# The last matrix product by seven products of halves, and input products in pairs of units

## The chip, the cores and the metric

One core of a Trainium2 chip runs the whole program. The metric is the time of one execution in microseconds (us) of device time. The engines are TensorE (PE, with its weight loads shown as PEld), VectorE (DVE), ScalarE (ACT), GpSimd (POOL) and SyncE (SP), which issues the transfers.

## The reference

Attention over 2 batches, 12 heads, 448 positions and head size 64 gives a matrix x of 896 tokens by 768. Two experts follow:

```python
scores = np.where(mask, -1e9, scale * q @ k.T);  x = softmax(scores) @ v
h = x @ w_in;  x = (h - np.tanh(h)) @ w_out              # first expert, d_ff 2048
a = x @ w_a;   b = x @ w_b;   out = (a * b) @ w_out2     # second expert, d_ff 1536
```

Everything is float32. The weights arrive as 8-byte words, whose bits the kernel unpacks on the chip.

## The kernel before

**Precision.** Each float32 operand is split into a high and a low half in the fp32r type: ACT casts the high half (`wh<-t`, line 244, for weights; line 601 for activations), DVE subtracts to get the low half (line 253; line 602). A product of two such operands takes three matmuls (high by high, high by low, low by high), all issued in line 280. A matmul covers 128 rows of depth, 128 output rows and 448 token columns, which are one batch.

**Weights.** SP loads a tile of 768x128 weights in two transfers (line 170). ACT casts its upper bits (`top<-raw`, line 179), DVE puts the bits together (`t<-raw,top`, line 193), and then the tile is split as above. The weight buffers hold five pairs of split tiles ahead of PE.

**Seven products.** Where a product is done on a 2x2 grid of blocks (two output blocks by two depth halves of the weights, two depth halves by two batches of the tokens), it takes seven block products instead of eight. They carry the numbers 1, 2, 5, 3, 6, 7, 4. The sums of blocks that they need are DVE work: `combine` for weights (lines 213 to 219), `minus` for tokens (line 605). A *unit* is one such 2x2 grid of weights. Each of the seven products of a unit of the second expert's input is 9 matmuls. The results stay in PSUM banks (tags s, o, t, h), into which later products of the unit go on adding. Before that, ACT copies some of them out (line 733), and DVE adds (line 697).

**Second expert, input.** Twelve units (six of w_a, six of w_b, in turn). `in_turn` sets the order of their products: unit after unit, 2, 6, 5, 7, 3, 4, with product 1 of the next unit ahead of 4. `times` (line 722) multiplies a by b into twelve g tiles.

**Second expert, output.** 768 output columns are six blocks, taken two at a time. Of the depth of 1536, the first 768 go by the seven products (`seven`), the second 768 by ordinary products (`rest`): for each two blocks 7x9 + 4x18 = 135 matmuls. The tokens' terms for it come from `early_terms`, `late_terms` and `split_wide`; `kept` (line 858) copies a result out of PSUM, and `put` stores it.

The order of the instructions from the first expert on is set by the framework's scheduler, which moves instructions that are ready ahead of others on each engine. On the chip every engine works through its own list in order.

Of the kernel before, what the change touches and what calls it, by code (L numbers as in the profile page):

```python
# [9 lines left out]
F32 = mybir.dt.float32  # L10
F32R = mybir.dt.float32r
# [40 lines left out]
def attention_moe_moe2(ctx, tc, q, k, v, w_in, w_out, w_a, w_b, w_o, out):  # L52
# [20 lines left out]
    PARTS = KD  # L73
    NK = KD // 2
    WB = 5
    scale = 1.0 / float(D) ** 0.5

    const = ctx.enter_context(tc.tile_pool(name="const", bufs=1))
# [30 lines left out]
        units.append(len(tiles))  # L109
        tiles.extend([block(w, slice(0, DM), f), block(w, slice(0, DM), f + 1)])  # L110

    def in_turn(u0, early):

        n = len(units) - u0
        out = [(0, 1), (0, 5), (1, 1), (1, 5)] if early else [(0, 1)]
        for u in range(n):
            ms = [2, 5, 6, 3, 7, 4] if early and u == n - 1 else [2, 6, 5, 7, 3, 4]
            for m in ms:
                if m == 4 and u + 1 < n:
                    out.append((u + 1, 2 if early and u == 0 else 1))  # L120
                out.append((u, m))
        seen = set()
        stages.append([(u0 + u, m) for u, m in out if not ((u, m) in seen or seen.add((u, m)))])
        plan.extend(stages[-1])

    f0 = 0
    for g in GROUPS1:
# [9 lines left out]
        for dm in range(KD) if f0 < DFF1 // 128 else DM_ORDER:  # L137
            whole(block(w_out, slice((f0 - g) * 128, f0 * 128), dm))
    u0 = len(units)
    for f in range(0, NF2, 2):  # L140
        for w in (w_a, w_b):
            pair(w, f)
    in_turn(u0, True)
    for dm in range(0, KD, 2):
        pair(w_o, dm)
        u = len(units) - 1
        plan.extend((u, m) for m in (1, 5, 2, 3))
        whole(block(w_o, slice(DM, 2 * DM), dm))
        plan.extend((u, m) for m in (6, 7))
        whole(block(w_o, slice(DM, 2 * DM), dm + 1))  # L150
        plan.append((u, 4))
    last_use = {}
    for j, (i, m) in enumerate(plan):
        for x in (i,) if m is None else (units[i], units[i] + 1):
# [3 lines left out]
    thirds, summed = {}, set()  # L158

    def load_part():  # L160

# [20 lines left out]
    def bits():  # L182

        i = at["bits"]
        while at["t"] in last_use and last_use[at["t"]] < at["halve"]:
            at["t"] += 1
        if i >= at["abs"] or i >= at["t"] + TP:
# [4 lines left out]
        ts[i] = tp.tile([128, KD, 128], I32, tag="t", name="t")[:, 0:nk]  # L192
# [3 lines left out]
        at["bits"] += 1  # L196

    def source(j):

        i, m = plan[j]  # L200
        if m is None:
            return ts[i].bitcast(F32)
        if m == 7:
            return thirds[i]
        t = ts[units[i] + int(m in (4, 5))].bitcast(F32)
        return t[:, 3:6] if m in (2, 3, 4) else t[:, 0:3]

    def combine(u, m):
# [5 lines left out]
        elif u not in summed:  # L214
# [3 lines left out]
            nc.vector.tensor_tensor(out=a21, in0=a21, in1=a22, op=ALU.add)  # L218
            nc.vector.tensor_tensor(out=a11, in0=a21, in1=a11, op=ALU.subtract)

    def split_high():
        j = at["high"]
        if j >= len(plan):
            return
        i, m = plan[j]
        full = m is None
        if not full and j > at["halve"]:
            return
        if (i if full else units[i] + int(m not in (1, 2))) >= at["bits"]:
# [7 lines left out]
        if m in (3, 5, 6, 7):  # L237
# [472 lines left out]
    def times(u, q, x, on_chip):  # L710

        f, b = u // 2 * 2 + q // 2, q % 2
        if u % 2 == 0:
# [3 lines left out]
                x = e  # L717
            left[q] = x
            return
        if f not in g32:  # L720
            g32[f] = g_full[0].tile([128, NT], F32, tag=("gwh", "gwl")[f // NK if f < KD else f % 2], name="g32")
        nc.vector.tensor_tensor(out=g32[f][:, BATCHES[b]], in0=x, in1=left.pop(q), op=ALU.mult)

    def turn(u, m, outcome):

# [5 lines left out]
        if m in (1, 6, 5):  # L731
            c = {1: c1, 6: c2, 5: z}[m][u] = etile()
            nc.scalar.copy(out=c, in_=o)  # L733
        elif m == 4:
            outcome(u, 2, o, False)
        else:
# [55 lines left out]
            for _ in terms:  # L792
                pass

    last, wide = [{} for _ in range(NK)], {}

    def early_terms(kk):

        g1, g2 = g32[kk], g32[kk + NK]
        t = [partp.tile([128, NT], F32R, tag="part", name="gpart") for _ in range(2)]  # L800
        last[kk][1], last[kk][5] = [[x[:, cs] for x in t] for cs in BATCHES]
        halve(*last[kk][1], g1[:, B0])
        minus(g1[:, B0], g1[:, B1], g1[:, B0])
        halve(*last[kk][5], g1[:, B0])
        minus(g1[:, B1], g2[:, B1], g1[:, B1])

    def roomy(f):

        if f == NF2 - 1:
            return small(2)  # L810
        pool, tags = (xp, ("xh", "xl")) if f < KD + NK else (xtra, ("th", "tl"))
        t = [pool.tile([128, NT], F32R, tag=x, name=x) for x in tags]
        return [[x[:, cs] for x in t] for cs in BATCHES]

    def split_wide(cs):

        for f in range(KD, NF2):
            if f not in wide:
                wide[f] = roomy(f)
            halve(*wide[f][cs.start // S], g32[f][:, cs])  # L820

    def late_terms():

        for kk in range(NK):
            t = [xp.tile([128, NT], F32R, tag=x, name=x) for x in ("xh", "xl")]
            last[kk][2], last[kk][3] = [[x[:, cs] for x in t] for cs in BATCHES]
        for m, cs in ((2, B0), (3, B1)):
            for kk in range(NK):
                halve(*last[kk][m], g32[kk + NK][:, cs])
        for kk in range(NK):  # L830
            g2 = g32[kk + NK]
            minus(g2[:, B1], g2[:, B1], g32[kk][:, B0])
            minus(g2[:, B0], g2[:, B0], g2[:, B1])
        split_wide(B0)
        for kk in range(NK):
            last[kk][7], = small()
            halve(*last[kk][7], g32[kk][:, B1])
        for m, cs in ((6, B1), (4, B0)):
            for kk in range(NK):
                t = g_full[0].tile([128, NT], F32R, tag="gwh", name="gwh")  # L840
                last[kk][m] = [t[:, x] for x in BATCHES]
                halve(*last[kk][m], g32[kk + NK][:, cs])
            if m == 6:
                split_wide(B1)

    def seven(o, m, go_on=False, done=1):

        wh, wl = next_weights()
        product(o, [((wh[:, kk], wl[:, kk]), last[kk][m]) for kk in range(NK)], go_on=go_on)
        at["done"] += done  # L850
        advance()

    def rest(w, o, cs, go_on=True):
        product(o, [((w[0][:, f - KD], w[1][:, f - KD]), wide[f][cs.start // S]) for f in wide], go_on=go_on)

    def kept(o):
        r = etile()
# [12 lines left out]
    for dm in range(0, KD, 2):  # L870
        o1, o5, o2, o3 = [next_bank()[:, :S] for _ in range(4)]
        seven(o1, 1)
        r0 = kept(o1)
        seven(o5, 5)
        r3 = kept(o5)
        seven(o2, 2)
        seven(o5, 3, True)
        w = next_weights()
        rest(w, o2, B0)
        add(r0, o2)  # L880
        put(dm, B0, r0)
        seven(o1, 6, True, 0)
        r1 = kept(o1)
        rest(w, o5, B1)
        add(r1, o5)
        put(dm, B1, r1)
        at["done"] += 3
        advance()
        seven(o1, 7, True)
        add(r3, o1)  # L890
        w = next_weights()
        rest(w, o3, B1, False)
        add(r3, o3)
        put(dm + 1, B1, r3)
        seven(o1, 4, True, 0)
        rest(w, o1, B0)
        put(dm + 1, B0, kept(o1))
        at["done"] += 4
        advance()
        advance()  # L900


_INS = ["q", "k", "v"]
# [24 lines left out]
```

## Time and profile before

| | us |
|---|---|
| median of 3 runs (lowest, highest) | 558.43 (558.07, 561.26) |
| the profiled execution's own time | 559.96 |
| its span, from the first instruction to the last | 558.2 |
| PE busy | 548.0 (98%) |
| DVE busy | 425.1 (76%) |
| ACT busy | 331.0 (59%) |

PE's busy time counts overlapping matmuls once. The attention takes the first 110 to 120 us, the first expert runs until about 318 us, the second expert's input product from there to the 480s (its end and the last product's start are interleaved), the last product to 554.9 us. A last copy and a last store end the span. The granted clock of PE is 1.00 throughout, the higher of its two levels (2.4 GHz).

### The profile page before, as it was taken

To read this page: it belongs to the slowest core of one execution; us is meant where nothing else is said; L and a number is where in the kernel's file an instruction comes from. 1 tells how busy PE (TensorE), PEld (TensorE's weight loads), DVE (VectorE), ACT (ScalarE), POOL (GpSimd) and SP (SyncE) were. 2 spreads that over 40 slices of the span, in tenths; PEclk is the share of its full clock that TensorE was granted. 3 is DMA by queue.
4 is the path that set the end of the run, shared out by engine and by line. 5 is a ranking of instruction groups with operands and counts; after the bars stand their busy time and mean duration, and the time that the engine had idled before them with its cause. 6 is when DMAs were issued, how large, how long until landed. Compare 5 with 4: busy or idle time off the path is not lost.

```text
span 558.2 us, 8730 instructions
## 1 busy us (share of the span) xinstructions
PE 548.0 (98%) x3121; PEld 486.3 (87%) x3121; DVE 425.1 (76%) x876; ACT 331.0 (59%) x706; POOL 65.8 (12%) x88
## 2 busy tenths in 40 slices
PE   8999999998999999999999999999999999999997
PEld 4777788897999899899899889999999999999996
DVE  6897886479988867549879988979788699985311
ACT  6997996457677843238756464665554558754120
POOL 5688672200000000000000000000000000000000
PEclk9999999999999999999999999999999999999999
DMA  8825350067133742313741115335343533432001
GB/s 259 249 83 150 89 147 1 1 189 225 56 115 116 234 129 86 112 57 99 218 136 57 54 60 178 112 106 169 104 132 105 169 100 100 138 109 90 34 33 49
DMA packets 70827, 64.94 MB, mean 116 GB/s; under 512 B 13952, under 2 KB 70784, under 8 KB 70784
## 3 DMA queue, kind: packets, MB, share of 16 engines
q1 hardware_dynamic: 70784, 64.40, 37.0%
q8 instruction: 24, 0.39, 0.3%
q14 instruction: 19, 0.16, 0.1%
HBM read 61.63 MB, written 2.75 MB: 115 GB/s over the span
## 4 chain that ended last, share of the span: by engine, by line
PE 90%; DVE 3%; DMA 3%; ACT 2%; issue 1%; SPq 0%; DVEq 0%; ACTq 0%
PE s L280 37%; PE t L280 20%; PE h L280 13%; PE o L280 8%; PE o L432 4%; PE s L371 4%; PE t L406 3%; ACT p L392 1%; DMA raw<-in_moe_w_out 1%; PE t L451 1%; PE h L406 1%; DVE xsum L637 1%; DVE t L193 1%; DMA v<-in_v 1%; DMA raw<-in_moe_w_in 1%
## 5 line engine op out<-in xcount | busy, mean ns | idle before, releaser
L244 ACT CAST wh<-t 128x384 fp32r<-128x384 f32 (+2 forms) x154 | 81.9, 562 | 86.0 <-PE s L280 37.7
L179 ACT CAST top<-raw 128x768 f16<-128x768 bf16 (+1 forms) x70 | 73.8, 1054 | 44.7 <-DVE t L193 11.8
L253 DVE TENSOR_TENSOR wl<-t,wh 128x384 fp32r<-128x384 f32 (+2 forms) x149 | 87.0, 605 | 17.4 <-ACT wh L244 17.2
L193 DVE SCALAR_TENSOR_TENSOR t<-raw,top 128x768 int32<-128x768 int32 (+1 forms) x70 | 68.8, 985 | 4.0 <-ACT top L179 3.7
L280 PE MATMUL s<-xl,wh 128*128 128x448 f32 x150 | 55.0, 367 | 0.0
L280 PE MATMUL s<-xh,wl 128*128 128x448 f32 x150 | 54.7, 366 | 0.0
L280 PE MATMUL s<-xh,wh 128*128 128x448 f32 x150 | 54.2, 367 | 0.2 <-ACT e L733 0.2
L392 ACT ACTIVATE p<-p,m 112x448 f32<-112x448 f32 (+3 forms) x96 | 49.9, 524 | 5.6 <-DVE m L383 5.3
L697 DVE TENSOR_TENSOR e<-s,e 128x448 f32<-128x448 f32 x33 | 20.4, 620 | 31.8 <-PE s L280 31.5
L383 DVE CUSTOM_DVE_ANT_0 p<-s,mask 112x448 f32<-112x448 f32 (+3 forms) x96 | 37.9, 441 | 7.3 <-PE s L371 6.7
L280 PE MATMUL s<-gwl,wh 128*128 128x384 f32 (+2 forms) x96 | 34.9, 365 | 0.3 <-DVE gwl L558 0.3
L280 PE MATMUL s<-gwh,wl 128*128 128x384 f32 (+2 forms) x96 | 34.9, 365 | 0.0
L280 PE MATMUL s<-gwh,wh 128*128 128x512 f32 (+2 forms) x96 | 34.3, 364 | 0.0
L280 PEld LDWEIGHTS s<-xh,wh 128*128 128x128 f32 x150 | 28.2, 188 | 2.9 <-ACT e L733 0.6
L280 PEld LDWEIGHTS s<-xh,wl 128*128 128x128 f32 x150 | 28.2, 188 | 2.3
L280 PEld LDWEIGHTS s<-xl,wh 128*128 128x128 f32 x150 | 28.2, 188 | 2.3
L406 PE MATMUL t<-ident,p 112*112 112x112 f32 x195 | 27.6, 265 | 0.2 <-POOL qkh L351 0.2
L432 PE MATMUL o<-pt,v 112*64 112x224 f32 (+1 forms) x288 | 26.7, 326 | 0.9 <-DMA v<-in_v 0.9
L414 ACT COPY pt<-t 112x448 f32<-112x448 f32 (+1 forms) x39 | 18.4, 483 | 14.8 <-PE t L406 12.8
L432 PEld LDWEIGHTS o<-pt,v 112*64 112x64 f32 x288 | 19.1, 136 | 8.3 <-issue 1.1
L280 PE MATMUL h<-xh,wh 128*128 128x448 f32 x69 | 25.8, 374 | 0.0
L280 PE MATMUL h<-xh,wl 128*128 128x448 f32 x69 | 25.7, 372 | 0.0
(213 smaller groups left out, 1442.2 us busy)
## 6 DMA issues: line engine op xcount, KB each, us to landing
raw<-in_moe_w_out SPq DMA_DIRECT2D x48, 383.2 KB, 3.8
raw<-in_moe_w_in SPq DMA_DIRECT2D x32, 383.2 KB, 4.2
raw<-in_moe_w_a SPq DMA_DIRECT2D x24, 383.2 KB, 3.9
raw<-in_moe_w_b SPq DMA_DIRECT2D x24, 383.2 KB, 3.7
raw<-in_moe_w_out SPq DMA_DIRECT2D x12, 255.5 KB, 4.3
qk<-in_q SPq DMA_DIRECT2D x12, 224.0 KB, 3.3
qk<-in_k SPq DMA_DIRECT2D x12, 224.0 KB, 4.0
v<-in_v SPq DMA_DIRECT2D x24, 112.0 KB, 3.5
```

The source lines that it names most:

```text
L179: nc.scalar.copy(out=tops[i % len(tops)][:, 0:nk, :, 1], in_=top[:, :, :, 2])
L193: nc.vector.scalar_tensor_tensor(out=ts[i], in0=low[:, :, :, 0], scalar=13, in1=top, op0=ALU.logical_shift_right, op1=ALU.bitwise_or)
L244: nc.scalar.copy(out=halves[j][0], in_=x)
L253: engine.tensor_tensor(out=lo, in0=source(j), in1=hi.bitcast(F32), op=ALU.subtract)
L280: nc.tensor.matmul(o, a, b_, start=j == 0 and not go_on, stop=j == n - 1, skip_group_check=True)
L371: nc.tensor.matmul(sc[i, c][e], a[r, 0, cs], b_[r, 1, :n], start=x == 0, stop=x == len(terms) - 1)
L383: nc.vector.tensor_tensor_reduce(out=p[:, e], in0=s, in1=mask[:QC, S - n:], scale=-scale, scalar=3.0e38, op0=ALU.add, op1=ALU.min, accum_o ...
L392: nc.scalar.activation(out=p[:, e], in_=p[:, e], func=ACTF.Exp, bias=least[i][:, c, e:e + 1], scale=-1.0, accum_out=sums[i][:, c, e:e + 1],)
L406: nc.tensor.transpose(out=pst[:QC, x * QC:(x + 1) * QC], in_=blk, identity=ident[:QC, :QC])
L414: nc.scalar.copy(out=out_, in_=in_)
L432: nc.tensor.matmul(o[64 * e:64 * e + 64, cs], vt[:, k_, e, :], p.rearrange("s c q -> s (c q)"), start=k_ == 0, stop=k_ == 2 * h + 1, skip_ ...
L697: nc.vector.tensor_tensor(out=x, in0=o, in1=x, op=ALU.add)
```

## The change

The last product takes all of its depth by seven products. Its unit is now one 2x2 grid of 768x128 tiles, so each of the seven is 18 matmuls; three units cover the six output blocks. The product number is the outer loop (`for m in LAST: for n, u in enumerate(quads)`): product 1 for the three units, then product 2 for the three, and so on. The tokens' terms are made by `term()`, 21 in all, each a cast and a subtraction over 896 columns, 12 of them after a `minus` over 896 columns; three come before the last unit's product 7, one after the input products, and the others one to three at a time behind the last product's own steps. Six of the twelve weight tiles of the last product are loaded and unpacked among the last units of the input product, into the buffers called part.

The input products of the second expert run in pairs of units: each of the seven products for one unit and then for the other. In the first pair the order is 1, 5, 2, 3, 6, 7, 4, in the others 1, 2, 5, 6, 3, 7, 4.

```diff
-    def in_turn(u0, early):
+    def in_turn(u0, pairs_):
...
+        if pairs_:
+            out = [(v, m) for u in range(0, n, 2) for m in (PAIR_FIRST if u == 0 else PAIR) for v in (u, u + 1)]
...
+    LAST = (1, 2, 5, 3, 6, 7, 4)
...
     for f in range(0, NF2, 2):
         for w in (w_a, w_b):
             pair(w, f)
+            n = len(units) - 1 - u0 - FIRST_LAST
+            if 0 <= n < KD:
+                of_last(n // 2, 1, n % 2, "part")
     in_turn(u0, True)
-    for dm in range(0, KD, 2):
-        pair(w_o, dm)
...
+    plan.extend((u, m) for m in LAST for u in quads)
...
+    def combine_quad(u, m):
...
+        if m == 3:
+            less(quad(u, 1, 1), quad(u, 2, 1), quad(u, 1, 1))
+            less(quad(u, 1, 2), quad(u, 1, 2), quad(u, 1, 1))
+        elif m == 7:
+            less(quad(u, 1, 1), quad(u, 2, 2), quad(u, 1, 1))
...
+    def term():
...
+        x = {1: b11, 2: b21, 5: b11, 3: b22, 6: b11, 7: b12, 4: b21}[m]
+        if m == 5:
+            minus(b11, b12, b11)
...
+        t = [pool.tile([128, NT], F32R, tag=x, name="last") for x in tags]
+        halve(*t, x)
+        last[m, p] = t
...
+    def all_of(u, m, o, go_on=False):
...
+        parts = [((wh[:, k], wl[:, k]), [x[:, BATCHES[k % 2]] for x in last[m, k // 2]]) for k in range(KD)]
+        product(o, parts, go_on=go_on)
+        at["done"] += 2
...
     for u, m in stages[-1]:
-        if u - u0 == NF2 - 1 and m in (2, 5, 6):
-            early_terms({2: 0, 5: 1, 6: 2}[m])
         turn(u, m, lambda u, q, x, on_chip: times(u - u0, q, x, on_chip))
-    late_terms()
...
+        if u - u0 == NF2 - 1 and m == 3:
+            for _ in range(NP):
+                term()
+    last_turned.append(True)
+    term()
+    acc = {}
+    for m in LAST:
+        for n, u in enumerate(quads):
+            if m in (1, 2, 5):
+                acc[n, m] = bank({1: "sss", 2: "tto", 5: "sht"}[m][n])[:, :S]
+            o = acc[n, {6: 1, 7: 1, 4: 1, 3: 5}.get(m, m)]
+            all_of(u, m, o, m in (3, 6, 7, 4))
+            if m == 1:
+                c1[n] = kept(o)
+            elif m == 2:
+                add(c1[n], o)
+                put(2 * n, B0, c1[n])
+            elif m == 5:
+                z[n] = kept(o)
...
+            for _ in range(AHEAD[n]):
+                term()
+            advance()
```

PE's list has 2977 matmuls and transposes before and 2950 with the change; all that goes away is in the last product, 405 before and 378 now. On DVE, 878 instructions become 857.

At the start of the second expert's input product, PE's list before reads as follows. `s<-x` is at first the end of the first units' product 5, whose result ACT then copies out; the last row here is the first matmul of product 3 into the same bank, which waits for that copy.

```order
L280 MATMUL s<-xl,wh 128x448
L280 MATMUL s<-xh,wl 128x448
L280 MATMUL s<-xl,wh 128x448
L280 MATMUL s<-xh,wl 128x448
L280 MATMUL t<-gh,wh 128x448
L280 MATMUL t<-gl,wh 128x448
L280 MATMUL t<-gh,wl 128x448
L280 MATMUL s<-xh,wh 128x448
```

With the change this stands there, after the end of product 5 of the two units (banks o and s):

```order
L328 MATMUL o<-xl,wh 128x448
L328 MATMUL o<-xh,wl 128x448
L328 MATMUL s<-xl,wh 128x448
L328 MATMUL s<-xh,wl 128x448
L328 MATMUL s<-th,wh 128x448
L328 MATMUL s<-tl,wh 128x448
L328 MATMUL s<-th,wl 128x448
L328 MATMUL s<-th,wh 128x448
L328 MATMUL s<-tl,wh 128x448
L328 MATMUL s<-th,wl 128x448
```

Six more matmuls (`t<-g`, `s<-g`) follow before the first `o<-xh`, so 14 matmuls instead of 5 lie between the end of product 5 and product 3 in the same bank.

In the last product, ACT's list with the change has this piece, where product 3 follows product 5 in a bank s (`last` are the tokens' terms, `tlast` weight tiles):

```order
L292 CAST wh<-tlast 128x768
L292 CAST wh<-t 128x768
L292 CAST wh<-tlast 128x768
L649 CAST last<-g_3822 128x896
L292 CAST wh<-tlast 128x768
L885 COPY e<-s 128x448
L292 CAST wh<-t 128x768
L885 COPY e<-h 128x448
```

The last cast of weights ahead of `COPY e<-s` waits for the matmul just before the end of product 5 of the first unit, the copy for that end; product 3 of the first unit begins 8 matmuls after that end in PE's list and waits for the copy. Before the change product 3 went on in the bank of product 5 too, with the 9 matmuls of product 2 written between them.

## Rows read from the trace of the kernel before

**Rows 1.** Page, part 1: engine, busy us (share of the span), instructions.

```profile
PE 548.0 (98%) x3121; PEld 486.3 (87%) x3121; DVE 425.1 (76%) x876; ACT 331.0 (59%) x706; POOL 65.8 (12%) x88
```

**Rows 2.** Windows of 10 us: busy PE, PEld, DVE, ACT, POOL; clock, DMA share, GB/s.

```profile
330.00:340.00 10.00, 9.77 (x49) 8.73 (x48) 9.15 (x17) 6.48 (x13) 0.00 (x0) 1.00 0.37 110
...
470.00:480.00 10.00, 10.00 (x51) 9.28 (x50) 10.00 (x18) 9.18 (x19) 0.00 (x0) 1.00 0.49 158
...
520.00:530.00 10.00, 10.00 (x50) 9.08 (x49) 3.15 (x5) 1.77 (x3) 0.00 (x0) 1.00 0.08 29
```

**Rows 3.** Timeline of PE, input product: start us, duration us, instruction.

```profile
379.79 0.36 PE L280 MATMUL t<-th,wl 128*128 128x448 f32 x1
...
419.51 0.36 PE L280 MATMUL s<-tl,wh 128*128 128x448 f32 x1
```

**Rows 4.** Timeline of PE at the start of the input product.

```profile
330.25 0.36 PE L280 MATMUL t<-gh,wl 128*128 128x448 f32 x1
...
330.84 0.47 PE L280 MATMUL s<-xh,wh 128*128 128x448 f32 x1 [0.23 <-ACT e L733]
...
331.15 0.37 PE L280 MATMUL s<-xl,wh 128*128 128x448 f32 x1
```

**Rows 5.** Timeline of PE and its weight loads in the last product.

```profile
498.55 0.36 PE L280 MATMUL s<-gh,wl 128*128 128x448 f32 x1
...
498.82 0.30 PEld L280 LDWEIGHTS t<-gwh,wh 128*128 128x128 f32 x2 [0.28 <-DVE e L697]
498.83 0.68 PE L280 MATMUL t<-gwh,wh 128*128 128x448 f32 x2
...
499.34 0.37 PE L280 MATMUL t<-gwh,wl 128*128 128x448 f32 x1
```

**Rows 6.** Timeline of PE from there to its last matmul.

```profile
500.79 0.37 PE L280 MATMUL t<-xh,wh 128*128 128x448 f32 x1
...
554.52 0.37 PE L280 MATMUL t<-gh,wl 128*128 128x448 f32 x1
```

**Rows 7.** Timeline of ACT at the end.

```profile
554.92 0.53 ACT L858 COPY e<-t 128x448 f32<-128x448 f32 x1 [13.93 <-PE t L280]
```

**Rows 8.** Timeline of DVE in the last product.

```profile
500.08 0.62 DVE L697 TENSOR_TENSOR e<-s,e 128x448 f32<-128x448 f32 x1
500.62 0.55 DVE L253 TENSOR_TENSOR wl<-t,wh 128x384 fp32r<-128x384 f32 x1
501.08 0.55 DVE L253 TENSOR_TENSOR wl<-s,wh 128x384 fp32r<-128x384 f32 x1
...
503.29 0.95 DVE L253 TENSOR_TENSOR wl<-t,wh 128x768 fp32r<-128x768 f32 x1
504.16 0.56 DVE L217 TENSOR_TENSOR s<-t 128x384 f32<-128x384 f32 x1
```

**Rows 9.** Groups by form: instructions of one tile, durations in ns least/median/most.

```profile
L637 DVE TENSOR_TENSOR xsum<-xh,xl x6: 1081/1086/1087, 114.0 to 137.3; 128x896 f32<-128x896 f32 x6
```

**Rows 10.** Timeline of ACT in the last product.

```profile
530.75 0.84 ACT L244 CAST wh<-t 128x768 fp32r<-128x768 f32 x1 [2.73 <-PE t L280]
531.49 0.96 ACT L858 COPY e<-t 128x448 f32<-128x448 f32 x2
```

**Rows 11.** Waits of ACT from 320 to 500 us: total us, times, longest.

```profile
ACT top L179 <- DMA raw<-in_moe_w_a: 5.1, 3, 3.4
```

**Rows 12.** Loads of weights, 330 to 500 us.

```profile
DMA to landing us min/median/max: 3.1/3.9/6.0
```

More of the change, by code (lines that the diff above doesn't have):

```diff
@@ L75, in attention_moe_moe2 @@
     WB = 5
+    AHEAD = (1, 0, 2)
+    FIRST_LAST = 5
+    PAIR_FIRST = (1, 5, 2, 3, 6, 7, 4)
+    PAIR = (1, 2, 5, 6, 3, 7, 4)
     scale = 1.0 / float(D) ** 0.5
@@ L110, in pair @@
         tiles.extend([block(w, slice(0, DM), f), block(w, slice(0, DM), f + 1)])
-    def in_turn(u0, early):
+    def in_turn(u0, pairs_):
         n = len(units) - u0
[L115 to L123, printed above, removed]
+        if pairs_:
+            out = [(v, m) for u in range(0, n, 2) for m in (PAIR_FIRST if u == 0 else PAIR) for v in (u, u + 1)]
+        else:
+            out = [(0, 1)]
+            for u in range(n):
+                for m in (2, 6, 5, 7, 3, 4):
+                    if m == 4 and u + 1 < n:
+                        out.append((u + 1, 1))
+                    out.append((u, m))
+        stages.append([(u0 + u, m) for u, m in out])
         plan.extend(stages[-1])
@@ L139, in attention_moe_moe2, with of_last @@
     u0 = len(units)
+    LAST = (1, 2, 5, 3, 6, 7, 4)
+    homes, quads = {}, {}
+    for n in range(KD // 2):
+        quads[u0 + NF2 + n] = {}
+    def of_last(n, r, f, home):
+        quads[u0 + NF2 + n][1 + r, 1 + f] = len(tiles)
+        homes[len(tiles)] = home
+        tiles.append(block(w_o, slice(f * DM, (f + 1) * DM), 2 * n + r))
     for f in range(0, NF2, 2):
@@ L157, in attention_moe_moe2 @@
     at = {"load": 0, "abs": 0, "bits": 0, "high": 0, "halve": 0, "use": 0, "done": 0, "t": 0, "slots": 0}
-    thirds, summed = {}, set()
+    thirds, summed, last_turned = {}, set(), []
     def load_part():
@@ L184, in bits @@
         i = at["bits"]
-        while at["t"] in last_use and last_use[at["t"]] < at["halve"]:
+        while at["t"] in homes and homes[at["t"]] != "t" or last_use.get(at["t"], at["halve"]) < at["halve"]:
             at["t"] += 1
-        if i >= at["abs"] or i >= at["t"] + TP:
+        home = homes.get(i, "t")
+        held_ = sum(homes.get(x, "t") == "t" for x in range(at["t"], i))
+        if i >= at["abs"] or home == "t" and held_ >= TP or home in ("th", "tl") and not last_turned:
             return
@@ L191, in bits @@
         top = tops[i % len(tops)][:, 0:nk].rearrange("p k f w -> p k (f w)").bitcast(I32)
-        ts[i] = tp.tile([128, KD, 128], I32, tag="t", name="t")[:, 0:nk]
+        if home == "t":
+            ts[i] = tp.tile([128, KD, 128], I32, tag="t", name="t")[:, 0:nk]
+        else:
+            t = (partp if home == "part" else xtra).tile([128, NT], I32, tag=home, name="tlast")
+            ts[i] = t[:, 0:KD * 128].rearrange("p (k n) -> p k n", n=128)
         nc.vector.scalar_tensor_tensor(
@@ L196, in bits, with quad @@
         at["bits"] += 1
+        if home == "part" and i in [x[2, 2] for x in quads.values()]:
+            a21, a22 = [ts[i_].bitcast(F32) for x in quads.values() if x.get((2, 2)) == i for i_ in (x[2, 1], i)]
+            nc.vector.tensor_tensor(out=a21, in0=a21, in1=a22, op=ALU.add)
+    def quad(u, r, f):
+        return ts[quads[u][r, f]].bitcast(F32)
+    WHERE = {1: (1, 1), 2: (1, 2), 5: (2, 1), 3: (1, 2), 6: (1, 1), 7: (1, 1), 4: (2, 2)}
     def source(j):
@@ L202, in source @@
             return ts[i].bitcast(F32)
+        if i in quads:
+            return quad(i, *WHERE[m])
         if m == 7:
@@ L219, in combine, with less @@
             nc.vector.tensor_tensor(out=a11, in0=a21, in1=a11, op=ALU.subtract)
+    def combine_quad(u, m):
+        def less(o, a, b_):
+            nc.vector.tensor_tensor(out=o, in0=a, in1=b_, op=ALU.subtract)
+        if m == 3:
[3 more added lines that the diff above has]
+            less(quad(u, 1, 1), quad(u, 2, 2), quad(u, 1, 1))
     def split_high():
@@ L225, in split_high @@
         i, m = plan[j]
-        full = m is None
-        if not full and j > at["halve"]:
+        full = m is None or i in quads
+        if m is not None and j > at["halve"]:
             return
-        if (i if full else units[i] + int(m not in (1, 2))) >= at["bits"]:
+        if i in quads and m is not None:
+            need = quads[i][1, 1 if m == 1 else 2]
+        else:
+            need = i if full else units[i] + int(m not in (1, 2))
+        if need >= at["bits"]:
             return
@@ L236, in split_high @@
             at["pair"] = [w_p.tile([128, KD, 128], F32R, tag=x, name=x) for x in ("wh", "wl")]
-        if m in (3, 5, 6, 7):
+        if m is not None and i in quads:
+            combine_quad(i, m)
+        elif m in (3, 5, 6, 7):
             combine(i, m)
@@ L719, in times @@
             return
-        if f not in g32:
-            g32[f] = g_full[0].tile([128, NT], F32, tag=("gwh", "gwl")[f // NK if f < KD else f % 2], name="g32")
-        nc.vector.tensor_tensor(out=g32[f][:, BATCHES[b]], in0=x, in1=left.pop(q), op=ALU.mult)
+        p = u // 2, b
+        if p not in g32:
+            g32[p] = g_full[0].tile([128, NT], F32, tag=("gwh", "gwl")[b], name="g32")
+        nc.vector.tensor_tensor(out=g32[p][:, BATCHES[f % 2]], in0=x, in1=left.pop(q), op=ALU.mult)
+    early3 = {}
     def turn(u, m, outcome):
@@ L733, in turn @@
             nc.scalar.copy(out=c, in_=o)
+            if m == 6 and u in early3:
+                add(c, early3.pop(u))
+                outcome(u, 1, c2.pop(u), True)
+        elif m == 3 and u not in c2:
+            early3[u] = o
         elif m == 4:
@@ L793, in attention_moe_moe2 @@
                 pass
[L795 to L844, printed above, removed]
@@ L846, in seven @@
-    def seven(o, m, go_on=False, done=1):
-        wh, wl = next_weights()
[L849 to L854, printed above, removed]
+    NP = NF2 // 4
+    last, terms_at = {}, [0]
+    def term():
+        n = terms_at[0]
+        if n >= len(LAST) * NP:
+            return
+        terms_at[0] += 1
+        m, p = LAST[n // NP], n % NP
+        b11, b12, b21, b22 = g32[p, 0], g32[p, 1], g32.get((p + NP, 0)), g32.get((p + NP, 1))
+        x = {1: b11, 2: b21, 5: b11, 3: b22, 6: b11, 7: b12, 4: b21}[m]
+        if m == 5:
+            minus(b11, b12, b11)
+        elif m == 6:
+            minus(b11, b22, b11)
+        elif m == 7:
+            minus(b12, b22, b12)
+        elif m == 4:
+            minus(b21, b21, b11)
+        pool, tags = (xp, ("xh", "xl")) if n % 7 < 6 else (xtra, ("th", "tl"))
+        t = [pool.tile([128, NT], F32R, tag=x, name="last") for x in tags]
+        halve(*t, x)
+        last[m, p] = t
@@ L865, in attention_moe_moe2 @@
     for u, m in stages[-1]:
-        if u - u0 == NF2 - 1 and m in (2, 5, 6):
-            early_terms({2: 0, 5: 1, 6: 2}[m])
         turn(u, m, lambda u, q, x, on_chip: times(u - u0, q, x, on_chip))
-    late_terms()
[L870 to L900, printed above, removed]
+        if u - u0 == NF2 - 1 and m == 3:
[17 more added lines that the diff above has]
+                z[n] = kept(o)
+            elif m == 6:
+                c2[n] = kept(o)
+                add(c2[n], acc[n, 5])
+                put(2 * n, B1, c2[n])
+            elif m == 7:
+                add(z[n], o)
+                put(2 * n + 1, B1, z[n])
+            elif m == 4:
+                put(2 * n + 1, B0, kept(o))
+            for _ in range(AHEAD[n]):
+                term()
+            advance()
 _INS = ["q", "k", "v"]
```

12 lines of the change are left out of this document (5 added, 7 removed).

## The prediction, made before the change was run

> **What bounds the kernel now.** I read the engines' busy time first: PE is busy 548.0 of 558.2 us, DVE 425.1 [rows 1]. Then I read the windows of 10 us from 330 us on, the stretch that the change touches: in every window there PE is busy 10.00 of 10.00, except 9.77 in the one from 330 [rows 2], at the higher of its two clock levels (granted 1.00). DVE is at 10.00 from 470 to 480 and at 3.15 from 520 to 530, so it is full just before the last product and mostly idle in it. PE sets the time, and a change pays by fewer matmuls, by a shorter step from one to the next, or by removing a hold; it loses where DVE, ACT or a load comes too late.
>
> The step comes from the timeline. In the input product 196 steps lie between 379.79 and 419.51 us [rows 3]: 39.72/196 = 0.2027 us. In the last product 260 steps lie between 500.79 and 554.52 [rows 6]: 53.73/260 = 0.2067 us. The operands and shapes are of the same kind, so the same matmul costs 4.0 ns more there. The place where this begins is a hold: at 498.82 PE waited for a DVE addition in a bank t [rows 5], and from then on every step is the long one. A hold does not always do that: behind the hold at 330.84 [rows 4] the step is again 0.2027, for the 826 steps up to the next hold, (498.55 - 331.15)/0.2027.
>
> **The change, part by part.**
>
> *Matmuls.* The last product goes from 405 to 378. 27 x 0.2027 = 5.47 us, all on the path, since PE has no idle time there. The Trainium skill, page "TensorE: Matmul & The Clock Gate", section "Back-to-back issue gap", gives a step of N/2.4 + 2.5 ns, from which I estimate 189.2 ns for 448 columns; by it this term would be 5.11 us. The rows say 202.7 and 206.7, and they decide.
>
> *The hold at 330.* From 330.25 to 331.15 two steps took 0.90 us instead of 0.405: 0.50 us lost [rows 4]. PE waited for the copy of product 5 to begin product 3 in that bank, 5 matmuls behind. Now 14 lie between, 2.84 us. The last matmul ends 0.36 us after its start, and the copy takes 0.53 [rows 7]; even with two casts ahead of it, 0.74 each [rows 10], that makes 2.4, and it is in time. Gain 0.50.
>
> *The hold at 498.* Three steps took 0.79 instead of 0.608: 0.18 us [rows 5]. That bank's order is gone. Gain 0.18.
>
> *The long step.* If nothing holds PE from the input product to the end, the remaining matmuls of the last product go at 0.2027: some 270 x 0.0040 = 1.08 us. Nothing in the trace says what the long step is, only that it began at a hold. I take the gain from the nearest rows, those 826 steps without a hold, and keep zero, and a loss (below), for the range.
>
> *DVE.* It loses 21 instructions but gets longer ones: 33 over 896 columns for the tokens' terms, 30 subtractions and additions over 768 for the weights. Spacing when back to back [rows 8]: 384 columns 0.46, 448 columns 0.54, 768 columns 0.87. For 896 the duration is 1.086 [rows 9], less the same overlap of 0.08: 1.00. The tight stretch is the run that starts when the last unit's product 2 ends and must reach the last term of product 2, which waits for the last input result. In it DVE has 44 instructions: 2 of 384, 9 of 448, 18 of 768, 15 of 896, so 0.9 + 4.9 + 15.7 + 15.0 = 36.5 us. PE has 198 matmuls between these two points, 40.1 us. With 0.5 for the matmul's end and the hand-over, DVE is 3.1 us early. It would be late from 8% more per instruction on. Up to product 5's weights for the third unit, 9 more instructions (8.4 us) against 41 more matmuls (8.3 us), the slack stays at 3.0. After that the spacing of PE's needs is wider. So DVE hides, and the idle DVE of the last product [rows 2] is what pays for it.
>
> *Loads and SP.* Six of the last product's weight tiles (12 transfers) move ahead into the input product, so three tiles follow each other instead of two. They take 3.9 us to land in the median and 6.0 at most [rows 12]. ACT's cast of a tile's upper bits waits for them in order [rows 11]. They cost nothing while the copies queued behind that cast are in time: a copy of product 5, 6 or 7 is wanted 27 matmuls, 5.5 us, after its product ends. SP's stores now all come behind product 2, and only the end waits for one, as before.
>
> *One new hand-over.* In the last product, product 3 of the first unit begins 8 matmuls after product 5's end in the same bank. ACT's copy stands behind a cast over 768 that is released one matmul earlier. From that release: 0.36 for the matmul's end, 0.03 for the hand-over (from 554.52 + 0.37 to 554.92, [rows 6, 7]), 0.74 from the cast to the copy's start [rows 10], 0.53 for the copy, 0.03 again: 1.69 us. The weight load before the waiting matmul would start after 8 steps, 1.62. So it is some 0.1 us late. I take 0.1 as lost, bounds 0 and 0.3 (0.28 is the idle time in rows 5).
>
> *The end* is the same: one copy, one store.
>
> *Sum:* 5.47 + 0.50 + 0.18 + 1.08 - 0.10 = 7.1 us. The profiled execution took 559.96 us with a span of 558.2; it would come to 552.8 and 551.1. The median of the runs without a profile is 558.43, 1.5 below the profiled execution, and the forecast is set against it: **551.3 us**.
>
> **Rivals.**
>
> *The long step in the last product.* The hand-over above is a hold at the same kind of place as the one at 498. If it starts the long step, 231 matmuls follow: 0.9 us less gain, 552.4. For: one of the two holds above did it. Against: the other did not, and this one may be none.
>
> *The long step from the start.* If the step is 0.2067 from the beginning of the input product, about 830 matmuls pay 0.0040, 3.3 us, and the 1.08 is not gained. 27 x 0.2067 + 0.68 - 3.3 = 2.9: 555.5 us. Against: the start of the stretch is laid out as before, and there the step was short.
>
> *DVE without overlap.* The same 44 instructions by their full durations (0.55, 0.62, 0.95, 1.086) are 1.1 + 5.6 + 17.1 + 16.3 = 40.1 us; with 0.5 for the hand-over DVE would be 0.5 us late for product 2 and, 9 instructions on, 1.3 us. With the long step after it (1.0) the time is 551.3 + 2.3 = 553.6. The Trainium skill has a rule for this, page "VectorE: DVE Perf Modes", section "Terms" (DRAIN): the next operation can't issue until the pipe is empty. By it the time would be this one. Rows 8 speak against it, since a 0.55 us instruction is followed by the next after 0.46; but the long instructions that depend on each other, of which the new list has more, are not in rows 8.
>
> *ACT behind a load* (slower than before). With three tiles in a row a landing may grow by half, from 6.0 to 9.0 us. ACT's longest wait for a tile, 3.4 us [rows 11], is then 6.4. A copy behind it has 5.5 less 0.36 and 0.53, so 4.6 us, and PE stands 1.8. Six such tiles make 10.8 us: 562.1 us. It decides from 7.1/6 = 1.2 us of hold each, a landing of 8.4. For: transfers are issued together, and ACT is in order. Against: the engines' share is 0.49 in the busiest of the windows shown [rows 2], and no landing after 330 exceeds 6.0.
>
> *No gain:* a place that I did not see takes the sum back, 558.4. That the change does not do what it says is excluded for the count of matmuls, which PE's list shows.
>
> **How the numbers follow.** Forecast as summed 0.50; long step in the last product 0.17; long step throughout 0.10; DVE without overlap 0.10; ACT behind a load 0.08; no gain 0.05. One percent, about what a measurement of this kernel can tell from no change, is 5.6 us: below 552.8 is faster. The forecast lies there and about 0.7 of the second case, 0.62 together; I say 0.60. Slower by over 1% needs more than 564.0: the upper part of the load rival and of what I did not see, 0.06. The rest, 0.34, is within. The range runs from 550.5 (the forecast with no late hand-over and with a start that gains some tenths more) to 556.0 (the long step throughout), and leaves out the load rival and no gain, with a little below: 0.17.
>
> **What would show it.** Right: PE 10.00 busy in all windows from 330 to the last matmul, steps of 0.2027 in the last product, no idle note behind 318 us, DVE busy near 9 in the windows of the last product up to the last two products, and the end 7 us earlier. A step of 0.2067 shows one of the first two rivals, and the place where it begins which. Idle PE released by DVE in product 2 or 5 shows the third, idle PE released by an ACT copy with ACT waiting for `raw` the fourth. The forecast is wrong if PE has more than 1 us of idle time behind 318 us.

## The result, and the profile after

The changed kernel takes 552.12 us (median of 4 runs, 552.06 to 552.91) against 558.42 beside it, a ratio of 0.988 (95% interval 0.985 to 0.991). The forecast was 551.3. The profiled execution took 552.16 us with a span of 550.4.

First the busy times, which answer to [rows 1]:

```profile
PE 542.4 (99%) x3094; PEld 481.5 (87%) x3094; DVE 439.6 (80%) x855; ACT 335.5 (61%) x688; POOL 65.8 (12%) x88
```

PE lost 5.6 us of work, while DVE gained 14.5: the saving was bought with DVE time. Then the windows of 10 us, with the columns of [rows 2] (behind the window and its length stand PE, PEld, DVE, ACT and POOL, then clock, DMA share and GB/s):

```profile
330.00:340.00 10.00, 10.00 (x51) 9.26 (x51) 9.61 (x19) 5.78 (x11) 0.00 (x0) 1.00 0.49 158
470.00:480.00 10.00, 10.00 (x51) 9.27 (x50) 10.00 (x14) 3.22 (x6) 0.00 (x0) 1.00 0.01 3
...
490.00:500.00 10.00, 10.00 (x51) 9.19 (x50) 10.00 (x13) 5.70 (x8) 0.00 (x0) 1.00 0.12 46
...
520.00:530.00 10.00, 10.00 (x51) 9.28 (x50) 5.44 (x8) 4.32 (x6) 0.00 (x0) 1.00 0.20 71
```

PE is at 10.00 in every window from 330 to 540 us, and the view of its waits is empty behind 318 us. DVE is full from 460 to 510. One figure stands out: the weight loads at 9.19 in the window from 490, where all others from 330 to 540 us have 9.26 to 9.28. That is the new hand-over, 0.08 us of loading that came late.

The stretch of the change runs from the first matmul of the input product to the last matmul. In after:

```profile
317.06 0.36 PE L328 MATMUL t<-xh,wh 128*128 128x448 f32 x1
...
546.69 0.37 PE L328 MATMUL s<-last,wl 128*128 128x448 f32 x1
```

and in the trace of before, whose last row is the second of [rows 6]:

```profile
317.68 0.36 PE L280 MATMUL t<-xh,wh 128*128 128x448 f32 x1
```

The stretch took 554.52 - 317.68 = 236.84 us before and 229.63 after: **7.21 us less**, where the sum of the prediction was 7.1. No step in it is the long one, and no hold is left. This length is the best measure here: it came out at 236.84 and 236.83 in two executions of before, and at 229.63 twice in after, while the times of whole runs of one kernel spread by 0.9 to 5.4 us within a set.

### The profile page after: what moved, and what is told of

Same layout as the page of the kernel before. It is cut to its first block, busy times and chain, and to the rows that moved or that the text cites. A ratio compares the mean times of both kernels' runs of the same rounds, so it can differ in the third digit from the quotient of the medians.

```text
span 550.4 us, 8639 instructions
## 1 busy us (share of the span) xinstructions
PE 542.4 (99%) x3094; PEld 481.5 (87%) x3094; DVE 439.6 (80%) x855; ACT 335.5 (61%) x688; POOL 65.8 (12%) x88
## 4 chain that ended last, share of the span: by engine, by line
PE 89%; DVE 4%; ACT 3%; DMA 2%; issue 1%; SPq 0%; POOL 0%; DVEq 0%; ACTq 0%
PE s L328 41%; PE t L328 17%; PE h L328 13%; PE o L328 7%; PE o L480 4%; PE s L419 3%; PE t L454 3%; ACT p L440 2%; DVE t L214 1%; DMA raw<-in_moe_w_out 1%; DVE xsum L685 1%; PE t L499 1%; ACT pt L462 1%; DMA v<-in_v 1%; DMA raw<-in_moe_w_in 1%
## 5 line engine op out<-in xcount | busy, mean ns | idle before, releaser
L301 DVE TENSOR_TENSOR wl<-t,wh 128x384 fp32r<-128x384 f32 (+2 forms) x136 | 81.7, 623 | 14.6 <-ACT wh L292 14.1
L214 DVE SCALAR_TENSOR_TENSOR t<-raw,top 128x768 int32<-128x768 int32 (+1 forms) x62 | 60.4, 988 | 2.0 <-ACT top L194 1.8
L328 PE MATMUL s<-last,wh 128*128 128x448 f32 x168 | 48.4, 365 | 0.0
L328 PE MATMUL s<-xl,wh 128*128 128x448 f32 x120 | 44.0, 367 | 0.0
L328 PE MATMUL s<-xh,wl 128*128 128x448 f32 x120 | 43.5, 366 | 0.0
L328 PE MATMUL s<-xh,wh 128*128 128x448 f32 x120 | 43.5, 366 | 0.0
L328 PEld LDWEIGHTS s<-last,wh 128*128 128x128 f32 x168 | 31.5, 188 | 2.6
L328 PE MATMUL s<-last,wl 128*128 128x448 f32 x84 | 30.7, 365 | 0.0
L649 ACT CAST last<-g 128x896 fp32r<-128x896 f32 x21 | 19.0, 942 | 10.4 <-PE t L328 4.5
L401 POOL TENSOR_TENSOR qkl<-qk,qkh 128x448 fp32r<-128x448 f32 x22 | 25.2, 1148 | 1.0
```

Source lines behind the costliest of these rows:

```text
L214: nc.vector.scalar_tensor_tensor(out=ts[i], in0=low[:, :, :, 0], scalar=13, in1=top, op0=ALU.logical_shift_right, op1=ALU.bitwise_or)
L301: engine.tensor_tensor(out=lo, in0=source(j), in1=hi.bitcast(F32), op=ALU.subtract)
L328: nc.tensor.matmul(o, a, b_, start=j == 0 and not go_on, stop=j == n - 1, skip_group_check=True)
L401: nc.gpsimd.tensor_tensor(out=lo[:, x], in0=qk[i][:, x], in1=hi[:, x].bitcast(F32), op=ALU.subtract)
```

## The experiments

Stretch means that length. The times are medians of whole runs, in brackets where there was a single run.

| kernel | stretch begins | stretch, us | time, us |
|---|---|---|---|
| before | 317.68 | 236.84 | 558.42 |
| before, again | 315.54 | 236.83 | 558.35 |
| pairs only | 318.33 | 236.97 | 559.50 |
| last product only | 318.07 | 230.29 | 554.09 |
| before with 27 matmuls fewer | 318.39 | 231.26 | 553.76 |
| before with one addition fewer | 318.18 | 235.77 | (559.39) |
| after | 317.06 | 229.63 | 552.12 |
| after, again | 315.85 | 229.63 | 551.23 |
| after, 8 multiplications more | 318.07 | 236.22 | (559.72) |
| after, loads two tiles ahead | 317.23 | 230.54 | (553.21) |
| after, early tiles loaded twice | 315.95 | 232.40 | (554.04) |
| after, one copy more | 316.04 | 230.07 | (551.57) |

**1. Before, again.** No edit.

> The kernel before, unchanged, profiled once more. Theory A (the forecast counted the long step although it was only in the profiled execution, 559.96 us, and not in the median of 558.42): the profile shows the last product at 0.2027 us a step, no 0.5 us wait on a load of k at 4.5 us, holds of 0.50 near 330 and 0.18 near 498 as before, and an execution of some 558.4 (559.96 less 1.05 less 0.5). Rival B (the long step belongs to every execution of the old last product, and some 0.8 us of the gain was lost at another place): the last product again at 0.2067 over some 260 steps.

Measured: 558.35 us, the profiled run 557.80. Theory A fell at its main point. The wait for k at the start was indeed gone, but the long step was there again, from the same hold:

```profile
496.41 0.36 PE L280 MATMUL s<-gh,wl 128*128 128x448 f32 x1
496.69 0.67 PE L280 MATMUL t<-gwh,wh 128*128 128x448 f32 x2
497.19 0.37 PE L280 MATMUL t<-gwh,wl 128*128 128x448 f32 x1
...
552.37 0.37 PE L280 MATMUL t<-gh,wl 128*128 128x448 f32 x1
```

These are the rows of [rows 5, 6] shifted by 2.14 us, and 2.14 is what this execution was ahead at the start of the stretch. So what sets these two executions apart lies in the attention and the first expert, ahead of the change.

**2. The pairs alone.** The order `PAIR_FIRST`, `PAIR` and `early3` put into before, the old last product kept.

> Only the second expert's input products in pairs; the last product as before, 405 matmuls. Theory A: the hold of 0.50 us near 330 is gone, nothing else changes on PE: 558.42 - 0.50 = 557.9 us, the hold of 0.18 at the last product's start stays. Rival B (the paired order costs something of its own, by DVE, by ACT or by the loads, that the after kernel hides): 558.4 or more, with a wait of PE behind 318 us that the before kernel does not have.

Measured: 559.50 against 558.95, ratio 1.002 (1.000 to 1.004), a stretch of 236.97. Rival B. PE's timeline:

```profile
471.34 0.36 PE L283 MATMUL s<-gpart,wl 128*128 128x448 f32 x1
472.42 0.47 PE L283 MATMUL s<-xh,wh 128*128 128x448 f32 x1 [0.72 <-ACT wh L247]
472.73 0.36 PE L283 MATMUL s<-xl,wh 128*128 128x448 f32 x1
...
474.56 0.37 PE L283 MATMUL h<-gh,wl 128*128 128x448 f32 x1
475.55 0.47 PE L283 MATMUL h<-xh,wh 128*128 128x448 f32 x1 [0.62 <-ACT e L719]
475.85 0.36 PE L283 MATMUL h<-xl,wh 128*128 128x448 f32 x1
```

The holds of [rows 4] and [rows 5] are gone and so is the long step (0.50 + 0.18 + 1.08 = 1.76 us), but two new holds cost 1.08 - 0.20 + 0.11 = 0.99 and 0.89. At the first, PE waits for ACT's cast of weights of the old last product; at the second, the next matmul in PE's list goes on in the bank h that ACT has still to copy out. 236.84 - 1.76 + 1.88 = 236.96, and 236.97 was measured: the account closes.

**3. The last product alone.** In after, `in_turn` is put back to the order of before.

> Only the last product all by seven, 378 matmuls, with its weights loaded early as in the change; the input products in the order of before, unit after unit. Theory A: 552.12 + 0.50 (the hold near 330, back again) = 552.6 us, no other wait on PE, steps of 0.2027 in the last product. Rival B (the pairing is also what gives DVE its time before the last product): PE waits for DVE near the last product's product 2 and the time is above 553.5 us. Rival C (the hold costs nothing in the unprofiled runs): 552.1 us.

Measured: a stretch of 230.29, which is 0.66 above after; 554.09 us against 558.95, ratio 0.991 (0.989 to 0.994). The hold near 330 is back (0.39 + 0.11 in PE's timeline), and there is a little of rival B in the stretch. That the time is above rival B's 553.5 does not speak for more of it, since the sum of the two holds, 0.67, is all that the stretch has more than after:

```profile
493.27 0.36 PE L327 MATMUL h<-last,wh 128*128 128x448 f32 x1
493.54 0.47 PE L327 MATMUL t<-last,wh 128*128 128x448 f32 x1
493.54 0.19 PEld L327 LDWEIGHTS t<-last,wh 128*128 128x128 f32 x1 [0.28 <-DVE last L649]
493.85 0.36 PE L327 MATMUL t<-last,wl 128*128 128x448 f32 x1
```

PE waits for a term's low half from DVE, 0.17 us. So the last product alone is worth 6.55 of the 7.21; the pairs add 0.66 to it, and lose 0.13 without it. The step behind this hold stays 0.2027, though its rows look like those of [rows 5].

**4. The matmuls alone.** In before:

```diff
-    def rest(w, o, cs, go_on=True):
-        product(o, [((w[0][:, f - KD], w[1][:, f - KD]), wide[f][cs.start // S]) for f in wide], go_on=go_on)
+    def rest(w, o, cs, go_on=True, n=KD):
+        product(o, [((w[0][:, f - KD], w[1][:, f - KD]), wide[f][cs.start // S]) for f in list(wide)[:n]], go_on=go_on)
...
-        rest(w, o1, B0)
+        rest(w, o1, B0, n=NK)
```

> The kernel before with 27 matmuls of its last product left out (in the last product for the 4th quarter of each pair of row tiles, 9 of the 18 direct matmuls), so the output is wrong there; DVE, ACT and loads keep all their work. Theory A (PE alone sets the time): 27 x 0.2027 = 5.47 less, 552.95 us (27 x 0.2067 = 5.58 less, 552.85, if the long step is in every run). Rival B (the old last product is also held by DVE, ACT or stores, and fewer matmuls alone would not pay in full): above 553.5 us, with PE waiting in the last product.

Measured: a stretch of 231.26, so 5.58 less, which is 27 x 0.2067: this kernel has the long step too. The time was 553.76 against 558.95, ratio 0.991 (0.989 to 0.992). The time is above rival B's 553.5, but PE has no wait in the stretch beyond the two of before, so the stretch is as theory A has it. By the formula in the Trainium skill, page "TensorE: Matmul & The Clock Gate", section "Back-to-back issue gap", which is given there for an isolated matmul, an estimate would be 5.11; the trace does not agree.

**5. After, again.** No edit.

> The changed kernel as it is, timed beside the kernel before on one chip. The stretch from the second expert's first matmul to the last one took 236.84 and 236.83 us in two executions of before and 229.63 in one of after: 7.21 less. Theory A (all of it is in the time; the 6.30 between the first medians is the spread of the part ahead of 315 to 318 us): a difference of medians of 7.2, between 6.7 and 7.7, and again a stretch of 229.6. Rival B (the part ahead of the stretch became some 0.9 us longer in the changed kernel): 6.3, with the stretch starting about 1 us later than in most executions of before.

Measured: 551.23 against 558.87, ratio 0.985 (0.982 to 0.989), a stretch of 229.63 that begins at 315.85. That is theory A. The difference of medians, 7.64, is 0.43 above 7.21, and the first, 6.30, was 0.91 below. The stretch began between 315.5 and 318.4 us over all these executions, in both kernels. Rival B falls: the changed kernel does not begin it later.

**6. Before without one addition.**

```diff
-        add(r0, o2)
+        if dm:
+            add(r0, o2)
```

> The kernel before without one DVE addition, the first unit's product 1 plus product 2 in the last product (that part of the output is left out), so that bank t is free when the next product wants it and the hold of 0.18 us near 498 goes; PE's list is the same. Theory A (the long step is started by that hold): steps of 0.2027 to the end and a stretch of 236.84 - 0.18 - 1.08 = 235.6 us. Rival B (the long step belongs to the old last product's operands and has nothing to do with the hold): steps of 0.2067 from the same place, a stretch of 236.66.

Measured: 235.77, by neither theory.

```profile
499.05 0.37 PE L280 MATMUL s<-gh,wl 128*128 128x448 f32 x1
...
499.83 0.36 PE L280 MATMUL t<-gwh,wl 128*128 128x448 f32 x1
...
553.95 0.36 PE L280 MATMUL t<-gh,wl 128*128 128x448 f32 x1
```

The addition left out was not the one that PE waited for: the hold is still there, 0.17 us at 499.32 with the weight load 0.28 late behind an addition in bank t (three steps in 0.78). Yet the step behind it is 0.2027: 267 steps lie between the last two rows, 54.12 us. So the hold alone does not make the long step, nor do the old operands, and 1.07 less than before is the price of the long step by itself.

**7. DVE's room.**

```diff
+        for _ in range(9 if (u, q) == (NF2 - 1, 2) else 1):
             nc.vector.tensor_tensor(out=g32[p][:, BATCHES[f % 2]], in0=x, in1=left[q], op=ALU.mult)
```

> The changed kernel with the multiplication that ends the last input result done 8 times more, with the same result: 8 x 0.535 = 4.3 us more on DVE in the tight run, on the chain to the last term of product 2. In the trace of after that term is there 2.6 us before PE's first use. Theory A (2.6 us is DVE's real room): PE is held by about 1.7 us there, a stretch of 229.63 + 1.7 = 231.3, or 232.2 if a long step follows. Rival B (DVE has no room, as without overlap): 4.3 or more, 233.9. Rival C (the order gives way and nothing is held): 229.6.

Measured: 236.22, 6.59 more, worse than any theory. The eight on DVE, PE's timeline, and windows between the named times:

```profile
489.33 5.23 DVE L772 TENSOR_TENSOR g<-s,e 128x448 f32<-128x448 f32 x8
...
494.61 0.68 PE L328 MATMUL s<-last,wh 128*128 128x448 f32 x2 [3.71 <-DVE g L772]
...
496.74 0.57 PE L328 MATMUL o<-last,wh 128*128 128x448 f32 x1
497.11 0.57 PE L328 MATMUL s<-last,wh 128*128 128x448 f32 x1
...
499.32 0.36 PE L328 MATMUL t<-last,wl 128*128 128x448 f32 x1
```
```profile
496.00:498.90 2.90, 2.90 (x9) 2.60 (x8) 2.90 (x4) 2.90 (x5) 0.00 (x0) 0.50 0.00 0
499.40:502.00 2.60, 2.60 (x14) 2.36 (x13) 2.60 (x4) 2.29 (x4) 0.00 (x0) 1.00 0.00 0
```

The dose was larger than meant. The eight write to one place, and each begins 0.03 us after the end of the one before: (5.23 - 0.62)/7 = 0.66 us each and not 0.535, so 5.3 us and not 4.3. Three things add up. The hold is 3.87 + 0.10 us: the multiplications read bank s, which PE wants back, and the scheduler put three other DVE instructions between the first one and the eight, so this wait came before the one on the term (PE's list differs from that of after too, in 26 places). Then, some 1.2 us after PE began again, the granted clock was 0.50, the 1.2 GHz level, for nine matmuls at 0.37 us: some 1.55. Then the long step until the end, about 266 x 0.0040 = 1.06. So the run does not measure the room. What it does show of DVE is that the room is small: 5.3 us more are not hidden. The size of the room is read from the trace of after:

```profile
488.25 5.09 DVE L650 TENSOR_TENSOR last<-g,last 128x896 fp32r<-128x896 f32 x5
...
491.97 0.36 PE L328 MATMUL t<-last,wh 128*128 128x448 f32 x1
```

The first of the five is the low half of product 2's last term. It ends 1.08 us after its start, at 489.33, and PE uses it at 491.97: 2.6 us early.

**8. Loads two tiles ahead.** `at["bits"] + 3` becomes `+ 2` behind the attention.

> The changed kernel with weight tiles loaded two tiles ahead instead of three, behind the attention: each transfer starts one tile later. In after ACT waits for a tile 2.9 us at most and nothing of it reaches PE. Theory A (a copy behind such a wait has 4.6 us): ACT's longest wait rises by some 2 us to 5, PE is held by at most some 0.5 us at a few places, a stretch of 229.6 to 231. Rival B (ACT behind a load, the rival that would have made the change slower): waits of 6 us and more, PE held 1.8 us at six places, a stretch of 240.

Measured: ACT's longest wait for a tile is 3.0, almost what it was, so this did not test the load rival. PE has no hold. But the stretch is 230.54, 0.91 longer, and the place where it becomes longer is the new hand-over:

```profile
499.63 0.57 PE L328 MATMUL t<-last,wh 128*128 128x448 f32 x2
500.04 0.57 PE L328 MATMUL s<-last,wh 128*128 128x448 f32 x2
...
501.07 0.37 PE L328 MATMUL t<-last,wl 128*128 128x448 f32 x1
...
502.93 0.37 PE L328 MATMUL t<-last,wl 128*128 128x448 f32 x1
```

From 501.07 to 502.93 are 9 steps of 0.2067. Behind the matmul at 500.04 come 231 more, 231 x 0.0040 = 0.92. This is the first rival of the prediction, with its count (231 matmuls) and its price (0.9), in a kernel whose PE list is that of after. It was not there in the two executions of after, though the weight load of this hand-over was 0.11 us late in all three.

**9. Early tiles loaded twice.** `for _ in range(2 if homes.get(i) == "part" else 1)` ahead of the transfer.

> The changed kernel with the six early weight tiles of the last product loaded twice into the same place, second load behind the first: the transfers of these tiles land later, and those of the tiles behind them too. In after the landings from 320 to 460 have a median of 5.2 us and a longest of 6.8, and ACT waits 2.9 at most. Theory A (the rival of ACT behind a load is real, only its threshold, a landing of 8.4 us, was not reached): the doubled tiles land after 9 us and more, ACT waits 5 us and more for them, and PE is held at several of the six places behind ACT or DVE, 1 to 3 us each: a stretch of 232 to 245. Rival B (three buffers for the tiles give so much room that even this stays hidden): 229.6 to 230.6.

Measured: 232.40 us, two holds instead of six. ACT and then PE:

```profile
403.07 1.07 ACT L195 CAST top<-raw 128x768 f16<-128x768 bf16 x1 [4.37 <-DMA raw<-in_moe_w_b]
406.36 1.08 ACT L195 CAST top<-raw 128x768 f16<-128x768 bf16 x1 [1.44 <-DMA raw<-in_moe_w_b]
407.31 0.52 ACT L785 COPY e<-h 128x448 f32<-128x448 f32 x1
...
412.96 1.06 ACT L195 CAST top<-raw 128x768 f16<-128x768 bf16 x1 [3.44 <-DMA raw<-in_moe_w_out]
...
414.70 0.54 ACT L785 COPY e<-s 128x448 f32<-128x448 f32 x1
```
```profile
406.95 0.36 PE L329 MATMUL s<-gh,wl 128*128 128x448 f32 x1
407.88 0.47 PE L329 MATMUL h<-xh,wh 128*128 128x448 f32 x1 [0.57 <-ACT e L785]
...
413.26 0.37 PE L329 MATMUL o<-gh,wl 128*128 128x448 f32 x1
415.29 0.47 PE L329 MATMUL s<-th,wh 128*128 128x448 f32 x1 [1.67 <-ACT e L785]
```

A copy stands behind a cast that waits for a tile, and PE behind the copy: 0.83 and 1.94 us, 2.77 in all, which is the whole difference from 229.63. The mechanism of the load rival is real. It took six tiles loaded twice to bring it out; the longest landing was then 8.2 us, against 6.8 in after. The second hold came behind a wait of 3.44 us, so the room at that place is less than the 4.6 us that the prediction gave such a copy.

**10. One copy more at the hand-over.** `kept(o)` once more before `z[n] = kept(o)` for the first unit.

> The changed kernel with the copy of the first unit's product 5 made once more before the copy that is used: 0.43 us (the spacing of two such copies in the trace of after) more between that product and product 3 in the same bank; PE's list is the same. In after that hand-over has the weight load 0.10 us late and the matmul not at all. Theory A (the weight load's room is the only one): the load is 0.53 us late, the matmul about 0.33 later than its place, a stretch of 230.0, or 230.9 if the long step follows. Rival B (the copy is not what PE waits for there): 229.63.

Measured: 230.07, 0.44 more, by theory A.

```profile
498.44 0.57 PE L328 MATMUL t<-last,wh 128*128 128x448 f32 x2
499.17 0.30 PEld L328 LDWEIGHTS s<-last,wh 128*128 128x128 f32 x2 [0.54 <-ACT e L885]
499.17 0.69 PE L328 MATMUL s<-last,wh 128*128 128x448 f32 x2 [0.17 <-ACT e L885]
499.70 0.36 PE L328 MATMUL t<-last,wl 128*128 128x448 f32 x1
```

The matmul came 0.33 late, and 0.11 is lost behind it. No long step follows.

None of these has a shorter stretch than the changed kernel, and they point to no version that would: PE is busy in all of it, and a shorter one needs fewer matmuls again, from a DVE with 2.6 us of room where it is tightest.

## Why the prediction was right, point by point

*Matmuls, 5.47.* Right: 27 fewer alone gave 5.58, at the long step of before.

*The holds, 0.50 and 0.18.* Right: neither is in after, and the first returns when only the order of the input is put back (run 3).

*The long step, 1.08.* Right in size in these two traces (the four gains make 7.23, and 7.21 was measured), but the reason given was thin. It was read as what a hold leaves behind, to go with the hold. The runs show that a hold is not enough (runs 3 and 6) and that the changed kernel can have it too (run 8). The term is a chance that came out well, not a saving that is sure; the two rivals on it were rightly kept. Of the second, the long step from the start, nothing was seen: in all twelve executions of the table the step of the input product is 0.2027.

*The new hand-over, -0.10.* The mechanism was right, the size of the loss not. In after the load of the weights came late as worked out, from the row of 499.26 to that of 499.77, and the matmul behind it stood in its place:

```profile
499.26 0.39 PEld L328 LDWEIGHTS t<-last,wh 128*128 128x128 f32 x2
499.77 0.30 PEld L328 LDWEIGHTS s<-last,wh 128*128 128x128 f32 x2
...
499.46 0.57 PE L328 MATMUL t<-last,wh 128*128 128x448 f32 x2
499.87 0.57 PE L328 MATMUL s<-last,wh 128*128 128x448 f32 x2
```

From 499.46 to 499.87 are two steps of 0.2027. A load 0.1 us late is absorbed in both executions of after; with one copy more (run 10) it is not, and in run 8 the long step began behind it.

*DVE, 3.1 us early.* The trace says 2.6. The run from 452.24 to 489.33 has the 44 instructions as counted and takes 37.1 us instead of 36.5, since the sum put a wait at nothing: near its start DVE stood idle for 0.51 us behind a cast of ACT.

```profile
453.38 0.56 DVE L301 TENSOR_TENSOR wl<-t,wh 128x384 fp32r<-128x384 f32 x1 [0.51 <-ACT wh L292]
```

The price of 1.00 us for 896 columns was exact: the five in the row of run 7 take 5.09, and (5.09 - 1.08)/4 = 1.00. So the 0.08 overlap holds for long instructions too, as long as the next one does not wait for the one before; the trace of after has no such pair behind 318 us. In run 7 there are seven, and they have no overlap. The Trainium skill's page "VectorE: DVE Perf Modes", section "Terms" (DRAIN), has the next operation wait for an empty pipe; the five instructions of 896 columns do not agree, the eight multiplications of run 7 do. (Over 768 columns the trace has 33 additions and subtractions for the weights, not 30; no sum uses that count.)

*Loads.* They land later, but not late enough. After, 320 to 460 us, landing and ACT's waits, as [rows 11, 12]:

```profile
DMA to landing us min/median/max: 3.1/5.2/6.8
```
```profile
ACT top L194 <- DMA raw<-in_moe_w_b: 10.1, 6, 2.9
ACT top L194 <- DMA raw<-in_moe_w_a: 5.3, 4, 1.9
```

The median grew from 3.9 to 5.2 us and the longest from 6.0 to 6.8, not to 9.0. ACT's wait in total grew from 7.1 us (5.1 in [rows 11] and 2.0 for `in_moe_w_out`) to 17.2 (with 1.8 for the same), but its longest wait fell from 3.4 to 2.9, and none reached PE.

*From the trace to the median.* Here the 0.8 us between 551.3 and 552.12 arose. The profiled execution of before was taken to be 1.5 above the median for reasons that the change leaves alone. That was right (the stretch did not differ, run 1), but the medians of 3 and 4 runs carry the spread of the first 318 us: their differences were 6.30 and 7.64 us in two sets of runs, on either side of 7.21. In the second set a part of it goes with PE's mean granted clock: where that was 0.999 or 1.000, the medians are 558.23 (5 runs) and 551.18 (5 runs), 7.05 apart, and six of the 11 runs of before, but one of the six of after, had 0.996 or 0.997 and took longer than that.

## What to carry to other kernels

Where one engine is full from a point on, take the sum of a change against the length of that stretch in the trace and not against the median of a few runs, which carries the spread of everything ahead of it. Of two changes, each can take away a hold that the other has alone: the pairs without the new last product had two behind ACT and lost 0.13, the new last product without the pairs had one of 0.17 behind DVE, and together neither is there. And a helper at 100% for 50 us is no alarm while its last result is there before it is wanted; read how early, and know that more work on it can cost more than its own time (run 7: 5.3 us on DVE, 6.59 on PE).

## What was not expected of the hardware

**A long hold cost twice.** In run 7 PE had been idle for 3.7 us, ran on at the higher clock for some 1.2 us, then at the lower level for about 3.3 us (granted 0.50, steps of 0.37 instead of 0.20), and then at the higher again. In the stretch, holds with up to 1.7 us of idle time (run 9) were followed by no such drop. But the length of one idle time does not tell it all: in the attention, PE stands idle for 0.92 to 0.96 us near 40 us in all twelve executions, and in three of them (runs 2, 6 and 7) the granted clock then stood at 0.50 for a while from 41.3 to 41.8 us on. In run 2:

```profile
41.90:45.20 3.30, 3.30 (x21) 2.18 (x21) 2.73 (x11) 2.81 (x12) 2.15 (x4) 0.50 0.00 0
```

In the same window after has 1.00.

**A second steady step.** The same matmuls step at 0.2027 or 0.2067 us, at a granted clock of 1.00, each for hundreds of them. In before, runs 1, 4 and 8 the longer one began at a matmul whose weight load was late by 0.1 to 0.3 us while PE was still at work on the one before; in run 7 it came after the stretch at the lower clock. After the ten holds in which PE stood idle for 0.2 to 1.7 us it never began. But in runs 3, 6 and 9 and in both executions of after there was such a late load and the step stayed short; at the new hand-over it was 0.11 us late in after and in runs 5, 8 and 9 alike, and the long step came in run 8 alone. What decides it stays open.
